# Weight fetches, the X split of odd groups and the gate blocks, moved to other places of a hand-written order

## The chip, the cores and the metric

The kernel runs on one NeuronCore of a Trainium2 chip. The metric is the time of one execution on the device, in microseconds. The core has five engines, each with its own queue of instructions, worked off in order: TensorE (PE, matmuls, with its weight loads shown as PEld), VectorE (DVE), ScalarE (ACT), GpSimd (POOL) and SyncE (SP), which here issues nearly all transfers (DMAs). An instruction waits in its queue until the semaphores say that its inputs are written and its output buffer has been read; what stands behind it in the same queue waits as well.

## The reference

Two branches read the same x (2048 tokens, 512 columns, float32) and are mixed by a gate for each token:

```python
qkv = (x @ wqkv).reshape(B, S, 3, H, Dh)          # H = 32 heads of Dh = 16
scores = einsum("bhqd,bhkd->bhqk", q, k) * Dh ** -0.5
mask = (i - j >= 0) & (i - j < 256)               # causal, sliding window
a = (softmax(where(mask, scores, -1e9)) @ v) @ wo
b = (silu(x @ w_gate) * (x @ w_up)) @ w_down      # 1792 hidden columns
g = sigmoid((x * gate_w).sum(-1))
out = g * a + (1 - g) * b
```

## The kernel before

Every float32 product is made of three matmuls: each operand is split into a rounded part (hi) and the rest (lo), and hi x hi, hi x lo and lo x hi are added. A split is two instructions: a cast on one engine and a subtraction on another. For weights and for the projected Q and K (the X tiles) these are ACT and POOL, for w_down both are on DVE.

The heads are worked in 8 groups of four. After a prologue that makes V and the first groups' Q and K, the main loop runs over 128 slots `t`, 16 for each group, and one more; slot `t` holds one block of 128 keys of group `t // 16`. Each slot has four head steps `hd`. In a step PE does, for one head, the scores of the next group for the row maxima (stage1, L280), the scores of this group for the exps (stage2, L319), and three products of a projection (L230). DVE reduces the first to maxima (L282), ACT takes the exp of the second (L321) and POOL masks it (L323, L326). Group 7, from slot 112 (`g7`) on, has no stage1.

Four slots make a unit. In a unit PE makes two projections of 1024 tokens each, into the accumulators `pa` and `pb`: either both halves of the Q and K of a later group (`group_half`) or one gate and one up tile of the hidden layer (`gate_half`, `up_half`), whose results are kept in DRAM (`kept_h`, written at L547) and read again in the last phase. The first slot of a unit also holds some 86 small matmuls of av (exps times V, L343) after its second step, and so is longer. `finish` then normalises av on ACT (L358) and DVE and writes it out (od, issued by POOL).

Everything else is put into places by hand. `later(t, hd, f)` puts `f` behind the matmuls of step (t, hd), in the order in which it was called, and the order of the program is the order in each engine's queue. So a place has a time on PE; on SP, only the order against other issues counts. The places that matter here:

- `prepare` (L163, placed at L517 to L520): splits the weights that were fetched before (`PEND.pop(0)()`, cast L67 on ACT and subtraction L70 on POOL into `wh`, `wl`, two buffers each) and then issues the fetch of the next weights (`prefetch`, L75). There is one buffer `raw` for fetched weights, so that the issue on SP waits for POOL's subtraction of the split just before it. For weights whose first use is in slot t, the second of a unit, the split is at (t - 1, 1); for those of a unit's first slot, at (t - 2, 0) or as early as `wh` and `wl` are free.
- `group_half`, L550: ACT copies the accumulators to two `ev` buffers (a ring of five), and later splits them into the one pair of X tiles (`half`, casts L67 on ACT, subtractions L70 on POOL). `stack` (L263, L264) then issues 12 transfers from the X tiles to the Q and K tiles. The second half of a group can be split only when the first half's stack has read the X tiles.
- the gate: for each of 16 blocks of 128 tokens, `gate_fetch` (L594, SP) fetches the block of x to one of two buffers in turn, and `gate_block` (L597, DVE) multiplies it with gate_w and sums; the buffers are X tiles that no group needs any more. `gate_end` (L605 on, ACT and DVE) makes the gate of the sums.
- in group 7, `wd_early` fetches eight tiles of w_down (L75) to `ev` buffers, two in each unit, and splits them on DVE in the first slot of the next unit.
- `put_max` (L293 to L298) sends the row maxima by way of DRAM into the Q tiles: md on SP, and then q, which waits until md has landed.

At a unit's end DVE turns the accumulators of its projections into hidden tiles: two products for pa (L532) after two tanh of ACT (L529), and two for pb (L544). The next unit's matmuls need these accumulators again.

Of the kernel before, what the change touches and what calls it, by code (L numbers as in the profile page):

```python
# [19 lines left out]
NB = S // P  # L20
# [13 lines left out]
def gated_mix(ctx, tc, xT, xn, wqk, wv, wo, wgu, wd, gw, out):  # L34
# [70 lines left out]
    def halves_of(t):  # L105
        n = t.shape[-1] // 2
        return [t[:, :n], t[:, n:]]
# [49 lines left out]
    PEND = []  # L157
# [21 lines left out]
    with ExitStack() as A:  # L179
# [14 lines left out]
        def kept():  # L194
            return sm.tile([P, CH], F32, name="ev", bufs=EV)
# [3 lines left out]
        def x_pair(pool=None, name="x"):  # L199
            return tuple((pool or sm).tile([P, 2 * CH], F32R, name=f"{name}{w}", bufs=1) for w in ("hi", "lo"))  # L200

        def split_qk(g, hf, cc, raw):
            hi, lo = (t[:, cc * CH:(cc + 1) * CH] for t in X[g, hf])
            split(hi, lo, raw, *act)
# [53 lines left out]
        def stack(g, hf):  # L258
            for pr in range(2):
                q, k = (halves_of(t[g % 2][pr])[hf] for t in (QT, KT))  # L260
                hi, lo = (x[32 * pr:] for x in X[g, hf])
                for b, (qx, kx) in enumerate(((hi, hi), (hi, lo), (lo, hi))):
                    nc.sync.dma_start(q[b::4].bitcast(F32), qx[:32].bitcast(F32))  # L263
                    nc.sync.dma_start(k[b::4].bitcast(F32), kx[64:96].bitcast(F32))  # L264
# [3 lines left out]
        def stage1(g, qb):  # L268

            hf, b = divmod(qb, NB // 2)  # L270
            if b == 0:
                MX[g, hf] = sm.tile([P, 4, NB // 2], F32, name="mx")
            q0, k0 = qb * P, max(0, qb - 2) * P
            n = q0 + P - k0
            for hd in range(4):
                pr, j = divmod(hd, 2)
                r = slice(64 * j, 64 * j + 63)

                ps = ps2.tile([P, CH], F32, name="ps2") if g == 0 and pr else ps1.tile([P, CH], F32, name="ps1")
                nc.tensor.matmul(ps[:, :n], QT[g % 2][pr][r, q0:q0 + P], KT[g % 2][pr][r, k0:k0 + n],  # L280
                                 start=True, stop=True)
                mx = nc.vector.tensor_tensor_reduce(out=ps[:, :n], in0=ps[:, :n], in1=mask[:, 3 * P - n:],  # L282
                                                    scale=1.0, scalar=NEG, op0=ALU.add, op1=ALU.max,
                                                    accum_out=MX[g, hf][:, hd, b:b + 1])
                if g == 0:
                    BEHIND.append(mx)
                yield
# [198 lines left out]
        first = chain(*(stage1(0, b) for b in range(NB)))  # L486
# [5 lines left out]
        for n, turn in enumerate(turns):  # L492
            for m, _ in enumerate(turn, 3 * NK * n):
                at = [max(0, i - wait) * 2 * NB // (total - wait) for i in (m, m + 1)]
# [19 lines left out]
        def later(t, hd, *fs):  # L514
            AT.setdefault((t, hd), []).extend(fs)

        for n, key in enumerate(KEYS[:-1]):  # L517
            if n:
                t, free = FIRST[key], LAST.get(KEYS[n - 2], 0) + 1 if n > 1 else 0
                later(*((t - 1, int(n > 1)) if t % 4 else (max(t - 2, free), 0)), prepare)  # L520

        SIL = {}

# [26 lines left out]
        def group_half(t, g, hf):  # L550

            t0 = t + 3 + hf

            def done(ps):
                places = [kept(), kept()]
                for m in range(2):
                    later(t0, 2 * m, lambda m=m: nc.scalar.copy(places[m], ps[m]))

                def half(m):
                    if m == 0:  # L560
                        X[g, hf] = x_pair()
                    split_qk(g, hf, m, places[m])
                first = t0 + 3 * hf
                later(first, 3, lambda: half(0))
                later(first + 1, 1, lambda: half(1))
                later(max(first + 1, (g - 1) * NB) if hf else first + 1, 3, lambda: stack(g, hf))
            return done
# [17 lines left out]
        g7 = (G - 1) * NB  # L585
# [7 lines left out]
        def gate_fetch(b):  # L593
            nc.sync.dma_start(XG[2 + b % 2], xn[b * P:(b + 1) * P])  # L594

        def gate_block(b):
            nc.vector.scalar_tensor_tensor(XG[1], XG[2 + b % 2], 1.0, XG[0], op0=ALU.mult, op1=ALU.mult,  # L597
                                           accum_out=gate[:, b:b + 1])
# [9 lines left out]
            nc.vector.tensor_scalar(igate, gate, -1.0, 1.0, op0=ALU.mult, op1=ALU.add)  # L608

        pieces = [h for two in (QT[0], KT[0], QT[1], KT[1]) for t in two for h in halves_of(t)]  # L610
        later(g7 - 4, 1, gate_place)
        for b in range(NB):
            t = g7 - 4 + b // 4 * 4
            later(*((t, 1), (t + 1, 3))[b // 2 % 2], lambda b=b: gate_fetch(b))
            later(t + 1 + b // 2 % 2, 2 + b % 2, lambda b=b: gate_block(b))
        later(g7 + NB - 3, 0, gate_end)
        for m in range(NB // 2):
            wd_early(m)

# [17 lines left out]
        for t in range(G * NB + 1):  # L637
            g, i = divmod(t, NB)
# [216 lines left out]
```

## Time and profile before

| what | value |
|---|---|
| three runs, us | 834.81, 838.31, 838.81 (median 838.31) |
| the profiled execution, us | 840.53, span 838.8 |
| PE busy, share of the span | 98% |
| DVE, ACT, POOL busy | 63%, 48%, 42% |
| mean granted TensorE clock | 0.995 |
| ACT's X split waiting for stack transfers (k<-xhi) | 9.5 us in 5 waits |
| DVE's gate blocks waiting for their fetch (xlo<-xn) | 11.7 us in 9 waits |

A row of the timeline has the start in us from the span's start, the duration in us, the engine, the line, the operation, output<-inputs and, in brackets, how long the engine sat idle before it and what ended that. "x2" means two instructions shown as one. Rows with SPq are issues of transfers on SP; their duration is that of the issue, not of the transfer. A piece of the chain of waits has start, duration and what it was. A row of the windows has the stretch, its length, the busy time of PE, PEld, DVE, ACT and POOL (with counts), the granted clock, the DMA engines' share and GB/s.

### The profile page before, as it was taken

The numbers are of one execution on the slowest core, as the hardware profiler recorded it, in microseconds if no ns is written. First come the engines' busy times: TensorE is split into PE (matmuls) and PEld (weight loads), VectorE is DVE, ScalarE is ACT, GpSimd is POOL, SyncE is SP. The second block draws the span as 40 slices with busy tenths as digits, with TensorE's granted clock in tenths as the row PEclk, the third lists the DMA queues.
The fourth block names the chain that finished last, engine by engine and source line by source line (L and its number), as shares of the span: only waits on it lengthen the run. The fifth ranks groups of instructions, "written<-read, shape, count | busy, mean of one in ns | idle before, by whom it ended". The sixth has DMA issues, their size and how long they took to land.

```text
span 838.8 us, 21376 instructions
## 1 busy us (share of the span) xinstructions
PE 824.8 (98%) x8329; PEld 697.2 (83%) x8329; DVE 528.8 (63%) x1493; ACT 400.1 (48%) x831; POOL 352.9 (42%) x640
## 2 busy tenths in 40 slices
PE   8999999999999999999999999989999999999998
PEld 7888998888889878888889888867788888888886
DVE  6396787877787777787787688865665332321322
ACT  7323566565556565565556555544533312222231
POOL 7723456465446565455556545455431211011020
PEclk9999999999999999999999999998999999999999
DMA  8584424523514434242454252453466342251401
GB/s 288 166 234 128 127 86 112 162 78 114 154 57 134 114 119 145 59 150 74 112 161 134 71 170 82 140 173 111 164 213 208 108 126 75 81 159 43 157 15 50
DMA packets 52980, 105.98 MB, mean 126 GB/s; under 512 B 9936, under 2 KB 14672, under 8 KB 52880
## 3 DMA queue, kind: packets, MB, share of 16 engines
q1 hardware_dynamic: 48912, 90.73, 35.8%
q0 software_dynamic: 3968, 13.90, 4.6%
q8 instruction: 65, 1.06, 0.5%
q14 instruction: 35, 0.29, 0.1%
HBM read 47.45 MB, written 31.98 MB: 95 GB/s over the span
## 4 chain that ended last, share of the span: by engine, by line
PE 89%; DMA 5%; SPq 2%; DVE 1%; issue 1%; ACT 1%; POOL 0%; DVEq 0%; ACTq 0%
PE pa L230 21%; PE pb L230 20%; PE pb L343 6%; PE ps L86 6%; PE ps L85 6%; PE ps L87 6%; PE ps L280 6%; PE ps L319 4%; PE ps L343 2%; DMA xlo<-xn 2%; PE pb L210 2%; PE pb L86 2%; PE pb L85 2%; PE pb L87 2%; DMA k<-xhi 2%; PE pa L737 1%
## 5 line engine op out<-in xcount | busy, mean ns | idle before, releaser
L282 DVE CUSTOM_DVE_ANT_0 ps<-ps,mask 128x384 f32<-128x384 f32 (+2 forms) x512 | 270.6, 539 | 114.3 <-PE ps L319 53.0
L321 ACT ACTIVATE pt<-ps 128x384 f32<-128x384 f32 (+2 forms) x512 | 238.0, 475 | 140.0 <-PE ps L280 70.8
L323 POOL TENSOR_SCALAR_AFFINE_SELECT pt<-pt 128x256 f32<-128x256 f32 x256 | 107.0, 418 | 220.3 <-ACT pt L321 218.1
L319 PE MATMUL ps<-q,k 64*128 64x384 f32 (+2 forms) x512 | 159.8, 331 | 0.0
L280 PE MATMUL ps<-k,q 63*128 63x384 f32 (+2 forms) x512 | 158.8, 330 | 0.8 <-DVE mx L282 0.8
L230 PE MATMUL pa<-xhi,wh 64*128 64x512 f32 x512 | 118.4, 399 | 3.9 <-DVE ev L532 3.8
L230 PE MATMUL pa<-xlo,wh 64*128 64x512 f32 x512 | 116.8, 395 | 0.0
L230 PE MATMUL pa<-xhi,wl 64*128 64x512 f32 x512 | 115.7, 392 | 0.0
L230 PE MATMUL pb<-xhi,wh 64*128 64x512 f32 x512 | 113.2, 394 | 0.0
L230 PE MATMUL pb<-xhi,wl 64*128 64x512 f32 x512 | 112.2, 392 | 0.0
L230 PE MATMUL pb<-xlo,wh 64*128 64x512 f32 x512 | 112.1, 391 | 0.0
L70 DVE TENSOR_TENSOR hl<-got,hh 128x512 fp32r<-128x512 f32 x51 | 43.3, 851 | 98.3 <-ACT hh L67 98.3
L280 PEld LDWEIGHTS ps<-k,q 63*128 63x128 f32 x512 | 88.7, 185 | 16.4 <-issue 5.7
L326 POOL TENSOR_SCALAR_AFFINE_SELECT pt<-pt 128x256 f32<-128x256 f32 x224 | 100.5, 449 | 0.0
L319 PEld LDWEIGHTS ps<-q,k 64*128 64x128 f32 x512 | 90.3, 184 | 4.8 <-issue 0.8
L343 PE MATMUL ps<-pt,vg 64*32 64x320 f32 (+4 forms) x1408 | 76.3, 350 | 3.1 <-ACT pt L321 3.1
L343 PE MATMUL pb<-pt,vg 64*32 64x320 f32 (+3 forms) x1360 | 78.1, 355 | 0.0
L282 DVE DVE_READ_ACCUMULATOR2_ANT mx<- 128x1 f32 x512 | 71.9, 140 | 0.0
L230 PEld LDWEIGHTS pa<-xhi,wh 64*128 64x128 f32 x512 | 62.5, 186 | 11.1 <-DVE ev L532 6.7
L343 PEld LDWEIGHTS pb<-pt,vg 64*32 64x32 f32 x1360 | 47.2, 107 | 27.2 <-DVE mx L282 7.3
L230 PEld LDWEIGHTS pa<-xhi,wl 64*128 64x128 f32 x512 | 61.9, 185 | 5.9
L230 PEld LDWEIGHTS pb<-xhi,wh 64*128 64x128 f32 x512 | 59.6, 185 | 5.6
(161 smaller groups left out, 1553.6 us busy)
## 6 DMA issues: line engine op xcount, KB each, us to landing
kept_h<-ev SPq DMA_DIRECT2D x52, 256.0 KB
got<-kept_h SPq DMA_DIRECT2D x51, 256.0 KB
od<-o POOLq DMA_DIRECT2D x32, 256.0 KB, 3.7
raw<-wgu SPq DMA_DIRECT2D x28, 256.0 KB
q<-xhi SPq DMA_DIRECT2D x56, 128.0 KB
k<-xhi SPq DMA_DIRECT2D x56, 128.0 KB
vd<-vs POOLq DMA_DIRECT2D x8, 672.0 KB, 4.7
vg<-vd SPq DMA_DIRECT2D x32, 168.0 KB
```

The costliest lines, as they stand in the source:

```text
L70: lo_eng.tensor_tensor(out=lo, in0=src, in1=hi.bitcast(F32), op=ALU.subtract)
L85: nc.tensor.matmul(ps, lh, rh, start=start and i == 0, stop=False, skip_group_check=skip)
L86: nc.tensor.matmul(ps, lh, rl, start=False, stop=False, skip_group_check=skip)
L87: nc.tensor.matmul(ps, ll, rh, start=False, stop=stop and i == n - 1, skip_group_check=skip)
L230: mm = nc.tensor.matmul(ps[me], w[r], x[r], start=not second and i == 0, stop=bool(second) and i == n - 1)
L280: nc.tensor.matmul(ps[:, :n], QT[g % 2][pr][r, q0:q0 + P], KT[g % 2][pr][r, k0:k0 + n], start=True, stop=True)
L282: mx = nc.vector.tensor_tensor_reduce(out=ps[:, :n], in0=ps[:, :n], in1=mask[:, 3 * P - n:], scale=1.0, scalar=NEG, op0=ALU.add, op1=ALU.m ...
L319: nc.tensor.matmul(ps[:, :n], KT[g % 2][pr][r, k0:k0 + P], QT[g % 2][pr][r, k0:k0 + n], start=True, stop=True)
L321: BEHIND.append(nc.scalar.activation(pt[:, j, :n], ps[:, :n], AF.Exp, scale=SCALE))
L323: nc.gpsimd.affine_select(out=pt[:, :, :P], in_=pt[:, :, :P], pattern=[[0, 2], [1, P]], compare_op=ALU.is_ge, fill=0.0, base=0, channel_mu ...
L326: nc.gpsimd.affine_select(out=pt[:, :, 2 * P:], in_=pt[:, :, 2 * P:], pattern=[[0, 2], [-1, P]], compare_op=ALU.is_ge, fill=0.0, base=-1, ...
L343: nc.tensor.matmul(AV[g, c][h][32 * j:32 * j + 32, q0 - c * CH:q1 - c * CH], VG[4 * g + kb // 4][o, kb % 4, 17 * j:17 * j + 32], PT[g, kb, ...
```

## The change

Three edits, all to places.

1. At L517 the split and the next fetch get places of their own. The fetch moves from directly behind the split to (t, 0), where the split is at (t - 1, 1), and to two steps behind the split where that is in step 0.
2. In `group_half` the second half's two casts and subtractions move one slot later for odd groups. Their stack stays at the start of the next group's 16 slots.
3. The gate blocks, four to a unit, move from the units that start in slots 108, 112, 116 and 120 to those of 112, 116, 120 and 124. With u for the start of the unit, blocks and fetches stood and stand at:

| block of the unit | fetch before | block before | fetch after | block after |
|---|---|---|---|---|
| a | (u, 1) | (u+1, 2) | (u-1, 0) | (u+1, 0) |
| b | (u, 1) | (u+1, 3) | (u-1, 1) | (u+1, 2) |
| c | (u+1, 3) | (u+2, 2) | (u+1, 1) | (u+2, 1) |
| d | (u+1, 3) | (u+2, 3) | (u+1, 3) | (u+2, 3) |

`gate_place`, which fetches gate_w, moves from slot 108 to 110, and `gate_end` from (125, 0) to (127, 0). The w_down fetches and splits keep their places, at (u+1, 2) and (u+2, 2) and in the next unit's first slot.

```diff
@@ places of the weights
             if n:
                 t, free = FIRST[key], LAST.get(KEYS[n - 2], 0) + 1 if n > 1 else 0
-                later(*((t - 1, int(n > 1)) if t % 4 else (max(t - 2, free), 0)), prepare)
+                at = (t - 1, int(n > 1)) if t % 4 else (max(t - 2, free), 0)
+                later(*at, lambda: PEND.pop(0)())
+                later(*((t, 0) if t % 4 else (at[0], 2)), prefetch)
@@ def group_half
-                first = t0 + 3 * hf
+                first = t0 + (3 + g % 2) * hf
                 later(first, 3, lambda: half(0))
                 later(first + 1, 1, lambda: half(1))
                 later(max(first + 1, (g - 1) * NB) if hf else first + 1, 3, lambda: stack(g, hf))
@@ the gate
-        later(g7 - 4, 1, gate_place)
+        later(g7 - 2, 1, gate_place)
         for b in range(NB):
-            t = g7 - 4 + b // 4 * 4
-            later(*((t, 1), (t + 1, 3))[b // 2 % 2], lambda b=b: gate_fetch(b))
-            later(t + 1 + b // 2 % 2, 2 + b % 2, lambda b=b: gate_block(b))
-        later(g7 + NB - 3, 0, gate_end)
+            t, n = g7 + b // 4 * 4, b % 4
+            later(t + (-1, -1, 1, 1)[n], (0, 1, 1, 3)[n], lambda b=b: gate_fetch(b))
+            later(t + (1, 1, 2, 2)[n], (0, 2, 1, 3)[n], lambda b=b: gate_block(b))
+        later(g7 + NB - 1, 0, gate_end)
```

## The prediction

> **What bounds the kernel now.** I read the page first, then the chain of waits in order of time, then the timelines of each engine around the pieces of that chain that are not TensorE.
>
> ```profile
> span 838.8 us, 21376 instructions
> PE 824.8 (98%) x8329; PEld 697.2 (83%) x8329; DVE 528.8 (63%) x1493; ACT 400.1 (48%) x831; POOL 352.9 (42%) x640
> PEclk9999999999999999999999999998999999999999
> PE 89%; DMA 5%; SPq 2%; DVE 1%; issue 1%; ACT 1%; POOL 0%; DVEq 0%; ACTq 0%
> ```
>
> TensorE (PE) sets the pace, so a wait is worth only what it costs PE. The 98% hides stalls, since matmul ends are modelled. The start of a slot's first score matmul (L319) is the better clock: a unit is one long slot, which carries the av matmuls, and three short ones of about 3.5 us. I give positions as (slot, head step); the first slot of group 7, the last, is 112.
>
> The chain names two kinds of transfer. The first is a stack transfer (k<-xhi), on which ScalarE (ACT) waits with the X split of an odd group's second half:
>
> ```profile
> 175.33 0.33 PE L319 MATMUL ps<-q,k 64*128 64x384 f32 x1
> 181.50 0.34 PE L319 MATMUL ps<-q,k 64*128 64x384 f32 x1
> ...
> 192.07 0.33 PE L319 MATMUL ps<-q,k 64*128 64x384 f32 x1
> 199.91 0.33 PE L319 MATMUL ps<-q,k 64*128 64x384 f32 x1
> ...
> 326.74 0.33 PE L319 MATMUL ps<-q,k 64*128 64x384 f32 x1
> 334.58 0.33 PE L319 MATMUL ps<-q,k 64*128 64x384 f32 x1
> ...
> 460.17 0.33 PE L319 MATMUL ps<-q,k 64*128 64x384 f32 x1
> 467.68 0.33 PE L319 MATMUL ps<-q,k 64*128 64x384 f32 x1
> ```
>
> Slot 24 is an undisturbed long slot: 6.17 us. Slots 28, 60 and 92 (groups 3, 5, 7) take 7.84, 7.84 and 7.51: together 4.7 us over.
>
> The second kind is the gate blocks' transfer (xlo<-xn), which holds VectorE (DVE), and DVE frees the accumulators (pa) that the next unit's first matmuls need:
>
> ```profile
> 400.50 0.33 PE L319 MATMUL ps<-q,k 64*128 64x384 f32 x1
> 410.67 0.33 PE L319 MATMUL ps<-q,k 64*128 64x384 f32 x1
> ...
> 533.65 0.33 PE L319 MATMUL ps<-q,k 64*128 64x384 f32 x1
> 545.38 0.34 PE L319 MATMUL ps<-q,k 64*128 64x384 f32 x2
> 560.81 0.42 PE L319 MATMUL ps<-q,k 64*128 64x384 f32 x2
> 564.66 0.79 PE L230 MATMUL pa<-xhi,wh 64*128 64x512 f32 x1 [3.43 <-DVE ev L532]
> 573.02 0.35 PE L319 MATMUL ps<-q,k 64*128 64x384 f32 x2
> 582.51 0.44 PE L319 MATMUL ps<-q,k 64*128 64x384 f32 x1
> 588.79 0.33 PE L319 MATMUL ps<-q,k 64*128 64x384 f32 x2
> 598.15 0.36 PE L319 MATMUL ps<-q,k 64*128 64x384 f32 x2
> 605.17 0.33 PE L319 MATMUL ps<-q,k 64*128 64x384 f32 x2
> ```
>
> Unit 108: its three short slots take 545.38 - 533.65 = 11.73 us; its twin in group 4, unit 76, needs 410.67 - 400.50 = 10.17 for the same work. That is 1.5 over. Slot 116: 12.21 us against 6.28 in slot 120, 5.9 over: PE stood still for 3.43 us and then ran slow. Slot 124: 7.02, 0.7 over. So the last group loses 6.6, and all known stalls add to 4.7 + 1.5 + 6.6 = 12.8 us.
>
> **The change part by part.**
>
> X split of odd groups, one slot later. The two casts and two subtractions are the same; only their place moves, from (27,3) and (28,1) to (28,3) and (29,1) in group 3.
>
> ```profile
> 194.54 0.62 ACT L67 CAST xhi<-ev 128x512 fp32r<-128x512 f32 x1 [2.45 <-DMA k<-xhi]
> 198.18 0.59 ACT L358 COPY o<-ps 128x512 f32<-128x512 f32 x1 [1.74 <-PE ps L343]
> 198.66 0.50 ACT L321 ACTIVATE pt<-ps 128x384 f32<-128x384 f32 x1
> ```
>
> ACT stood for 2.45 us until the last of 12 stack transfers landed; the exps behind it on ACT kept the ps buffers and so PE. In its new place the cast comes behind the copy at 198.18 and two exps, four microseconds after that landing, or over two once the stall's 1.7 us is taken off. The wait is gone: 4.7 us. The new place costs at worst its overrun of a step: 0.62 + 0.50 against 3.48/4 = 0.87, 0.25 us, twice for three groups, 1.5 us if the two ps buffers did not take it up. The first half's casts already sit in such short slots beside an unstalled PE, so I take 0. The stack of that half starts at (32,3) as before; the evacuated tiles are held one slot longer, and the ring of five next needs them at slot 35. Even groups keep their place; I count nothing there.
>
> Weight transfers. An issue on SP has no slot of its own, only its turn in SP's queue, so the move matters only where it passes another issue. Most move past nothing. Behind a split at (24,1), (44,1) and so on the next weights now go out after the maxima transfers and the 12 stack issues instead of before. They leave some 8 us later, with seven or so slots to spare until their split; I take 0. The stack gains no more than the 0.4 us that one issue takes (the row of 554.87 below), because the maxima ahead of it wait for DVE in any case. In the last group the fetches at (112,1) and (120,1) no longer stand before the gate's fetches and wait there for POOL's subtraction.
>
> Gate blocks. Unit 108 loses four blocks (0.8 us of DVE each) with their waits: 1.5 us back. Units 112 to 124 get four each: a and b at the head of the second slot and its middle, c and d in the third. Fetches a and b go out two slots ahead. But c's buffer is free only after a, d's after b, and between the two issues SP now has a w_down fetch and two kept_h writes. The price of d comes from unit 120 as template, with times from its start at 582.51:
>
> ```profile
> 587.87 0.69 DVE L360 TENSOR_TENSOR o<-pb,o 128x512 f32<-128x512 f32 x1 [2.61 <-ACT o L358]
> 588.93 0.77 DVE L70 TENSOR_TENSOR k<-ev,k 128x512 fp32r<-128x512 f32 x1
> 595.48 0.83 DVE L597 SCALAR_TENSOR_TENSOR xhi<-xlo,xhi 128x512 f32<-128x512 f32 x1 [0.51 <-DMA xlo<-xn]
> 598.13 1.27 DVE L532 SCALAR_TENSOR_TENSOR ev<-ev,pa 128x512 f32<-128x512 f32 x2
> ```
>
> The two pieces of the chain that carry such a transfer, and SP's queue around them:
>
> ```profile
> 556.32 5.93 DMA xlo<-xn
> ...
> 593.63 3.67 DMA xlo<-xn
> ```
>
> ```profile
> 551.32 0.58 SPq L296 DMA_DIRECT2D md<-mtt  x1
> 553.85 0.98 SPq L298 DMA_DIRECT2D q<-md  x2
> 554.87 0.40 SPq L75 DMA_DIRECT2D ev<-wd  x1
> 555.31 0.91 SPq L547 DMA_DIRECT2D kept_h<-ev  x2
> 556.32 0.96 SPq L594 DMA_DIRECT2D xlo<-xn  x2
> ...
> 592.77 1.20 SPq L594 DMA_DIRECT2D xlo<-xn  x2
> ```
>
> DVE ends the second w_down split at +7.2 (588.93 + 0.77) in either kernel, held by the copy before 587.87. Block a then ends at +8.0 and c is issued, which lands 2.7 us later (592.77 to 595.48), at +10.7. SP goes on: c's issue 0.6, w_down 0.4, kept_h 0.9, so d leaves at +9.9. How long d takes lies between 3.67 us (the second of the pair of 592.77, issued behind one other transfer) and 5.93 us (that of 556.32, issued behind a w_down fetch and two kept_h writes). The second has the queue that d will have, so I stay near it: 5.3, and d lands at +15.2. Block d (0.8) and the two products (1.27) end at +17.25. PE wants pa at 598.15 + 0.3, +15.95. The stall is 1.3 us in slots 120 and 124; bounds 0 and 2.0.
>
> Unit 112 also has the maxima: SP holds from md (551.32) to q (553.85). Without the weights and gate fetches ahead of it md goes some 1.5 us earlier, but the weight fetch, 0.33 to issue and about 0.5 of queue, stands ahead of c. I take 2.2 for slot 116 (bounds 0.8 and 3.6). Unit 124 has no w_down fetch, which saves about a microsecond, but the gate's exp now stands on ACT ahead of the last two tanh and waits for block d, with the last exps and the transition behind it: 0.7 (0 to 1.5). Together 2.2 + 1.3 + 1.3 + 0.7 = 5.5 in place of 6.6: 1.1 us.
>
> A stall of 2.2 us is shorter than the one that slowed the clock; slots 28 and 60, 1.7 over, left it at full speed:
>
> ```profile
> 558.00:572.00 14.00, 10.57 (x112) 7.04 (x110) 5.10 (x10) 3.92 (x9) 2.97 (x7) 0.76 0.59 201
> ```
>
> In this window the granted clock was 0.76: 0.24 x 14 = 3.4 us lost. 2.2 is nearer 1.7 than 3.43, so no loss of clock is in the sum. In the Trainium skill, "TensorE: Matmul & The Clock Gate", Part 1 on the clock gate, the clock halves after a whole idle window of about 3.4 us, and the windows run freely. By that rule a stall of 2.2 us can never slow the clock, and my sum stays; at the upper bound of 3.6 it depends on the phase, and the rule would add the 3.4 us only in some executions.
>
> Sum: 4.7 + 1.5 + 1.1 = 7.3 us. Against the profiled execution's own 840.53 us (1.7 more than its span) that gives 833.2; against the median 838.31, 831.0. Of the runs before one stood at 834.81, so that 3.5 us come and go by themselves.
>
> **The rivals.**
>
> All waits go. If d lands at the lower bound, 9.9 + 3.7, DVE ends at +15.7 and nothing stalls: 838.3 - 12.8 = 825.5. For it: fewer issues stand between SP and the fetches than before; against it: each fetch c and d still waits for a block of its own unit.
>
> One loss of clock stays. Slot 116 stalls 3.6 and loses 3.4 more: 4.8 worse than the forecast, 835.8. For it: the queue ahead of c in unit 112 is the longest of the four, and that slot is where it happened.
>
> The moved split brings nothing, because the stacks go out later too or POOL, with its subtractions in short slots, holds the next av: 831.0 + 4.7 = 835.7. Against it: the landing at 194.3 is well ahead of the new place.
>
> Slower: the fetch of d is slower in every unit than that of 556.32 was in one. Its place is d's turn behind w_down and kept_h; it decides once the transfer takes over 7.4 us, for then each of the slots 116, 120 and 124 stands 3.4 us and loses clock, 5.9 each as slot 116 did. 17.7 + 0.7 against 6.6 is 11.8 lost; less 6.2 won elsewhere, 5.6 over: 843.9. For it: kept_h, w_down and the gate share one queue here in all four units. Against it: no transfer of a gate block in the chain took even 6 us.
>
> **How the numbers follow.** The forecast has 0.46 (its own range 828 to 834.5), all waits gone 0.20, one loss of clock 0.16, the split without effect 0.08, slower 0.10. A measurement tells about 0.5% from no change, 4.2 us: faster is under 834.1, slower over 842.5. Faster then holds most of the forecast, the first rival and a little of the two at 835.7: 0.70; slower 0.09; the rest, 0.21, is the same. The range reaches from 824.5, the first rival with 0.4 us for the stacks of two or three groups besides, to 837.0, past the two rivals at 835.7.
>
> **What would show it.** Slots 28, 60 and 92 near 6.2 us, and no wait of ACT's xhi cast on k<-xhi in odd groups. Unit 108's short slots near 10.2. In slots 116, 120, 124 a wait of PE's pa matmuls on DVE ev of 1 to 2 us each, DVE's block d released by xlo<-xn each time, and no dip in the clock row. The prediction is wrong if slot 116 still takes 12 us, if the weight split waits for its late fetch, or if PE waits in slots 29 or 30.

## The result, and the profile after

| | before | after |
|---|---|---|
| runs, median (lowest to highest), us | 838.53 (834.81 to 839.73), 6 runs | 830.1 (829.66 to 832.56), 6 runs |
| the profiled execution, us | 840.53, span 838.8 | 829.82, span 828.1 |

The ratio is 0.9914, with a 95% interval from 0.989 to 0.9938: faster by 8.4 us between the medians, against the 7.3 of the sum. Two executions of the experiments, one of 2851.78 us with edit 1 alone and one of 4006.33 us with d's fetch earlier, were disturbed and are left out of the medians. The page of the changed kernel, its lines in the order in which those of before were shown:

```profile
span 828.1 us, 21367 instructions
PE 820.1 (99%) x8329; PEld 697.0 (84%) x8329; DVE 531.5 (64%) x1493; ACT 399.8 (48%) x831; POOL 351.3 (42%) x640
PEclk9999999999999999999999999999999999999999
PE 93%; DMA 2%; DVE 1%; SPq 1%; issue 1%; ACT 0%; POOL 0%; DVEq 0%
```

The engines do the same work. The chain, which had 5% in transfers and 2% in SP's queue, has 2% and 1%, and the clock row has lost its one 8. The timeline of PE, changed kernel, at the first score matmul of the slots that the prediction followed, with one pa matmul between:

```profile
192.27 0.33 PE L319 MATMUL ps<-q,k 64*128 64x384 f32 x1
198.44 0.33 PE L319 MATMUL ps<-q,k 64*128 64x384 f32 x1
...
324.04 0.33 PE L319 MATMUL ps<-q,k 64*128 64x384 f32 x1
330.19 0.33 PE L319 MATMUL ps<-q,k 64*128 64x384 f32 x1
...
456.19 0.33 PE L319 MATMUL ps<-q,k 64*128 64x384 f32 x1
462.36 0.33 PE L319 MATMUL ps<-q,k 64*128 64x384 f32 x1
...
528.26 0.33 PE L319 MATMUL ps<-q,k 64*128 64x384 f32 x1
538.43 0.34 PE L319 MATMUL ps<-q,k 64*128 64x384 f32 x2
553.70 0.44 PE L319 MATMUL ps<-q,k 64*128 64x384 f32 x2
554.86 0.49 PE L230 MATMUL pa<-xhi,wh 64*128 64x512 f32 x1 [0.72 <-DVE ev L534]
560.58 0.34 PE L319 MATMUL ps<-q,k 64*128 64x384 f32 x2
570.05 0.82 PE L319 MATMUL ps<-q,k 64*128 64x384 f32 x2
577.81 0.35 PE L319 MATMUL ps<-q,k 64*128 64x384 f32 x2
587.17 0.38 PE L319 MATMUL ps<-q,k 64*128 64x384 f32 x2
593.33 0.34 PE L319 MATMUL ps<-q,k 64*128 64x384 f32 x2
```

Differences of these starts, beside those of before. The last stretch goes from the start of slot 127 (as the others, from its first L319 in the trace) to the end of the span.

| stretch | before, us | after, us | gained |
|---|---|---|---|
| slots 28, 60, 92 | 7.84, 7.84, 7.51 | 6.17, 6.15, 6.17 | 4.7 |
| slots 109 to 111 | 11.73 | 10.17 | 1.6 |
| slot 116 | 12.21 | 6.88 | 5.3 |
| slot 120 | 6.28 | 7.76 | -1.5 |
| slot 124 | 7.02 | 6.16 | 0.9 |
| start of slot 127 to the end | 227.46 | 228.67 | -1.2 |
| slot 48 | 7.27 | 6.08 | 1.2 |

These add to 11.0 us, and the spans differ by 10.7. Slots 71 and 72 take back the difference: 9.98 us together before, 10.32 after, and 10.3 to 10.4 in every kernel below that has edits 1 and 2; the runs leave open why. Slot 48 was most likely a chance of the one profiled execution of before: every kernel below, those with a single edit too, has 6.09 to 6.10 there. Without it 9.8 us of the table are the change's, in this pair of executions.

How the first kind of stall went shows on ACT where slot 28 ends, in the timeline of the changed kernel:

```profile
196.69 0.59 ACT L358 COPY o<-ps 128x512 f32<-128x512 f32 x1 [2.66 <-PE ps L343]
198.36 0.61 ACT L67 CAST xhi<-ev 128x512 fp32r<-128x512 f32 x1
```

The cast, which had waited 2.45 us for the stacks, now comes after the copy and has no bracket: it waits for nothing. The waits by engine, changed kernel (engine, what it is to write and its line, what it waited for: us in total, times, longest):

```profile
DVE xhi L599 <- DMA xlo<-xn: 11.9, 8, 2.6
...
PE pa L230 <- DVE ev L534: 1.3, 2, 0.7
PE pa L343 <- POOL pt L323: 1.1, 1, 1.1
```

DVE waits for the gate's blocks as long as before (11.9 us against 11.7); what has gone is that PE waited for DVE behind it, 1.3 us now against 3.8, and the longest 0.7 against 3.4. (Edit 1 adds two lines, so that in the kernels that have it L534, L549, L596, L599 and L607 are what L532, L547, L594, L597 and L605 were.)

### The profile page after: what moved, and what is told of

The parts are those of the page before. It is cut to its first block, busy times and chain, and to the rows that moved or that the text cites. A ratio compares the mean times of both kernels' runs of the same rounds, so it can differ in the third digit from the quotient of the medians.

```text
span 828.1 us, 21367 instructions
## 1 busy us (share of the span) xinstructions
PE 820.1 (99%) x8329; PEld 697.0 (84%) x8329; DVE 531.5 (64%) x1493; ACT 399.8 (48%) x831; POOL 351.3 (42%) x640
## 4 chain that ended last, share of the span: by engine, by line
PE 93%; DMA 2%; DVE 1%; SPq 1%; issue 1%; ACT 0%; POOL 0%; DVEq 0%
PE pa L230 23%; PE pb L230 22%; PE pb L343 7%; PE ps L86 6%; PE ps L87 6%; PE ps L85 6%; PE ps L280 6%; PE ps L319 4%; PE pb L210 2%; PE ps L343 2%; PE pb L86 2%; PE pb L87 2%; PE pb L85 2%; DMA xlo<-xn 2%; PE pa L739 1%; PE pb L739 1%
## 5 line engine op out<-in xcount | busy, mean ns | idle before, releaser
L319 PE MATMUL ps<-q,k 64*128 64x384 f32 (+2 forms) x512 | 160.2, 331 | 0.0
L319 PEld LDWEIGHTS ps<-q,k 64*128 64x128 f32 x512 | 90.7, 184 | 5.7 <-issue 0.8
L343 PE MATMUL ps<-pt,vg 64*32 64x320 f32 (+4 forms) x1408 | 75.0, 346 | 0.0
L343 PE MATMUL pb<-pt,vg 64*32 64x320 f32 (+3 forms) x1360 | 73.9, 350 | 0.0
L343 PEld LDWEIGHTS pb<-pt,vg 64*32 64x32 f32 x1360 | 46.4, 106 | 28.0 <-DVE mx L282 7.3
```

Source lines behind the costliest of these rows:

```text
L319: nc.tensor.matmul(ps[:, :n], KT[g % 2][pr][r, k0:k0 + P], QT[g % 2][pr][r, k0:k0 + n], start=True, stop=True)
L343: nc.tensor.matmul(AV[g, c][h][32 * j:32 * j + 32, q0 - c * CH:q1 - c * CH], VG[4 * g + kb // 4][o, kb % 4, 17 * j:17 * j + 32], PT[g, kb, ...
```

## The experiments

Called 1, 2 and 3: the weight fetches two or three steps behind their split, the X split of odd groups one slot later, and the gate blocks in the last group. My theory after the result: 2 gives the 4.7 us, 3 gives the rest, 1 gives nothing. The rival: 1 gives part of it, since it takes a waiting issue out of SP's queue ahead of the gate's fetches. Each kernel ran on one chip beside runs of the kernel before, whose medians on the chips lie within 1.2 us of each other; differences between kernels that ran on different chips carry that much doubt.

| kernel | median, us (lowest to highest) | before, us | ratio [95%] |
|---|---|---|---|
| 1 alone | 833.57 (832.4 to 835.23) | 838.9 | 0.9941 [0.9921, 0.9961] |
| 1 alone, again | 834.22 (832.28 to 836.05) | 837.78 | 0.9947 [0.9926, 0.9967] |
| 2 alone | 832.08 (831.31 to 833.71) | 838.9 | 0.9924 [0.9897, 0.9951] |
| 3 alone | 835.69 (833.89 to 838.23) | 838.9 | 0.997 [0.9953, 0.9986] |
| 2 and 3 | 829.38 (828.57 to 829.76) | 838.9 | 0.9888 [0.9863, 0.9913] |
| 1 and 2 | 827.8 (827.56 to 830.65) | 837.78 | 0.9885 [0.9843, 0.9927] |
| 1, 2 and 3, again | 829.85 (828.97 to 830.56) | 837.78 | 0.9899 [0.9866, 0.9931] |
| fetch d a step earlier | 827.93 (826.79 to 827.97) | 838.05 | 0.9874 [0.9848, 0.9899] |
| end of the gate later | 829.39 (829.24 to 830.15) | 838.05 | 0.9897 [0.9876, 0.9918] |
| three buffers | 825.81 (825.67 to 826.08) | 838.05 | 0.9854 [0.9829, 0.9878] |
| three buffers, end later | 825.06 (824.99 to 825.82) | 838.05 | 0.9846 [0.9825, 0.9867] |
| three buffers, old places | 827.04 (826.62 to 827.5) | 838.94 | 0.9858 [0.983, 0.9885] |

The slots that differ, from the starts of L319 in each kernel's trace, in us:

```
slot          before  1     2      3     2+3   1+2   1+2+3       d     end   three  three  three
                      again alone  alone             after/again first late  bufs   +late  old places
60            7.84  10.04   6.17   8.40  6.17  6.13  6.15/6.13   6.17  6.13  6.13   6.17   6.17
71 + 72       9.98   9.89  10.07   9.98  9.99 10.29 10.32/10.35  10.30 10.39 10.40  10.32  10.30
110 + 111     8.25   9.60   8.11   6.68  6.68  7.93  6.68/6.68   6.68  6.69  6.68   6.69   7.90
115           3.12   3.12   3.12   3.11  3.11  3.12  3.11/3.12   3.69  3.12  3.12   3.12   3.12
116          12.21   6.74  11.14   6.45  6.07  6.44  6.88/6.96   5.68  6.81  5.26   5.26   5.29
119           3.24   3.25   3.22   3.23  3.22  3.25  3.23/3.23   3.92  3.25  3.26   3.26   3.29
120           6.28   6.29   6.28   7.77  7.74  6.29  7.76/7.77   6.27  7.72  6.29   6.26   6.30
124           7.02   5.81   6.16   6.47  6.49  5.83  6.17/6.67   6.28  6.21  5.85   5.81   5.82
127 to end  227.46 227.45 227.35 229.12 228.66 227.38 228.67/.64 228.28 227.89 228.24 227.51 227.50
```

**Edit 1 alone.** Only L517 to L520 of the diff:

```diff
-                later(*((t - 1, int(n > 1)) if t % 4 else (max(t - 2, free), 0)), prepare)
+                at = (t - 1, int(n > 1)) if t % 4 else (max(t - 2, free), 0)
+                later(*at, lambda: PEND.pop(0)())
+                later(*((t, 0) if t % 4 else (at[0], 2)), prefetch)
```

> The kernel before with the moved weight fetches alone. Theory (each part works by itself: the X split gives 4.7 us, the gate's places the rest, the moved fetches next to nothing): 0 to 1.2 us faster than before, the 1.2 only if slot 48's stack wait (7.27 us against 6.1) went because the stack now stands ahead of the fetch. Slots 28, 60, 92 stay at 7.5 to 7.8, slot 116 near 12. Rival (the order on SP did the last group's part: the fetch at (112,1) no longer stands ahead of the gate fetches and the maxima): 3 to 5 us faster, slot 116 at 7 to 9 and no dip of the clock.

It took 833.57 us against 838.9, 5 us less by the ratio, so the theory that edit 1 gives nothing falls. The trace kept of it is that of the 2851.78 us and can't be read slot by slot. So it ran again on another chip:

> The moved weight fetches alone, once more, for a trace that can be read slot by slot. The time fell by 5 us where my theory gave at most 1.2. New theory (the rival of the first run): the fetch at (112,1) no longer stands ahead of the gate fetches and of md on SP, so the gate's fourth block comes 2 us or more earlier and slot 116 loses no clock: slot 116 at 7 to 9 us, slots 28, 60, 92 still at 7.4 to 8.4, the time 4 to 6 us under before. Other theory (the stack goes out earlier, and the X split waits less): slots 28, 60, 92 at 6.2 to 6.8, and slot 116 at 11 to 12.

834.22 against 837.78, ratio 0.9947: 4.4 us by the ratio. By the slots it is in slot 116, 12.21 to 6.74 (I had expected 7 to 9), and in slot 124, 7.02 to 5.81 (0.9 of these 1.2 are gone with edit 2 alone too). Slots 60 and 111 were longer in this one execution (10.04; 5.47 for 4.12), which at 836.05 lies 1.8 above its kernel's median. Slots 28 and 92, at 7.66 and 7.60, are much as before, so the other theory, that the X split waits less, is out. SP's issues in the last group, first the timeline of the kernel before, then that of edit 1 alone:

```profile
544.17 5.11 SPq L75 DMA_DIRECT2D raw<-wgu  x2
549.39 1.88 SPq L594 DMA_DIRECT2D xlo<-xn  x2
```

```profile
545.08 0.84 SPq L596 DMA_DIRECT2D xlo<-xn  x2
551.94 0.59 SPq L296 DMA_DIRECT2D md<-mtt  x1
553.95 0.99 SPq L298 DMA_DIRECT2D q<-md  x2
...
556.90 1.35 SPq L596 DMA_DIRECT2D xlo<-xn  x2
```

The subtraction on POOL that the issue of 544.17 waited for, in the timeline before:

```profile
547.65 1.28 POOL L70 TENSOR_TENSOR wl<-raw,wh 128x512 fp32r<-128x512 f32 x1 [0.19 <-ACT wh L67]
```

PE with edit 1 alone, where slot 116 begins:

```profile
562.99 0.42 PE L319 MATMUL ps<-q,k 64*128 64x384 f32 x2
564.00 0.49 PE L230 MATMUL pa<-xhi,wh 64*128 64x512 f32 x1 [0.60 <-DVE ev L534]
```

Before, the weight fetch stood in SP's queue until POOL had done the subtraction that frees `raw`; two gate fetches, the maxima and the second pair of gate fetches stood behind it. Counted from the start of slot 112 (545.38 before; 547.6 here, 15.4 ahead of 562.99), the first pair went out at +4.0 before and at -2.5 with edit 1, md at +5.9 and +4.3, the pair that decides at +10.9 and +9.3. PE's stall fell from 3.43 us to 0.60, and with it the loss of clock in this slot. Not all of these 2.8 us are the earlier issue. This is the first block of the deciding pair on DVE, before and with edit 1 alone:

```profile
562.28 0.91 DVE L597 SCALAR_TENSOR_TENSOR xhi<-xlo,xhi 128x512 f32<-128x512 f32 x1 [6.19 <-DMA xlo<-xn]
```

```profile
561.92 0.69 DVE L599 SCALAR_TENSOR_TENSOR xhi<-xlo,xhi 128x512 f32<-128x512 f32 x1 [3.98 <-DMA xlo<-xn]
```

It began at +16.9 before and at +14.4 with edit 1. Of these 2.5 us, 1.6 come from the issue; the rest is the transfer, 6.0 us from issue to block before and 5.0 here. (The last 0.3 of the 2.8 are the blocks, 0.91 against 0.69.) The faster transfer does not need the edit: with edit 2 alone, where the weight fetch stands as before, the pair left at +11.1 and took 4.8, and the stall was 2.28 us. So the order on SP is worth some 1.6 us of the stall, and with it the clock where a stall of the old length loses it.

**Edit 2 alone.**

```diff
-                first = t0 + 3 * hf
+                first = t0 + (3 + g % 2) * hf
```

> The kernel before with the later X split of odd groups alone. Theory: 4.7 us faster, slots 28, 60, 92 at 6.2 each, slots 29 and 30 unchanged at 3.48, everything in the last group as before. Rival (the split's new place costs in the short slots, or the wait goes on to the next reader): 0 to 3 us faster, with over 0.2 us more in slots 29 and 30.

0.9924, 6.4 us (4.1 to 8.6). Slots 28, 60 and 92 all have 6.17; slot 124 has 6.16 for 7.02, and slot 116 is still at 11.14. The interval takes in the 4.7 of one profile. That the median gain lies above it may be chance, or the length of this stall, which varies: without edit 2, slot 60 took 7.84, 8.40 and 10.04 in three kernels, the last with a loss of clock.

**Edit 3 alone.** The hunk of the diff from `gate_place` to `gate_end`, and nothing else:

```diff
-        later(g7 - 4, 1, gate_place)
+        later(g7 - 2, 1, gate_place)
...
-        later(g7 + NB - 3, 0, gate_end)
+        later(g7 + NB - 1, 0, gate_end)
```

> The kernel before with the new places of the gate alone. Theory: 3.5 to 6 us faster: 1.5 from unit 108, and slots 116, 120, 124 at 6.2 to 8 with the clock full, less 1.4 at the end. Rival (the order on SP did it): slot 116 still over 9 us with a dip of the clock, and the time within 1.5 us of before.

0.997, 2.5 us, less than the 3.5 to 6 that I expected. It mends slot 116 (6.45) and slots 110 and 111 (1.6 together), and pays 1.5 in slot 120 and 1.7 at the end; slot 60 took 8.40 in the profiled execution.

**Edits 2 and 3, without edit 1.** The changed kernel with

```diff
-                at = (t - 1, int(n > 1)) if t % 4 else (max(t - 2, free), 0)
-                later(*at, lambda: PEND.pop(0)())
-                later(*((t, 0) if t % 4 else (at[0], 2)), prefetch)
+                later(*((t - 1, int(n > 1)) if t % 4 else (max(t - 2, free), 0)), prepare)
```

> The changed kernel with the weight fetches back behind their splits. Theory: within 1.2 us of the changed kernel (830.1), on the slower side if slot 48 goes back to 7.3. Rival (the order on SP did the last group's part): 3 to 6 us slower than the changed kernel, with slot 116 over 9 us.

829.38, ratio 0.9888, where the changed kernel has 0.9914 and 0.9899: the intervals overlap. Slot 116 is even shorter, 6.07. Beside the other two, edit 1 adds nothing that can be told.

**Edits 1 and 2, without edit 3, and the changed kernel again beside it.** The first is the diff without the hunk of edit 3, the second the changed kernel unaltered.

> The changed kernel with the gate back in its old places (moved fetches and later X split only). If the moved fetches alone take the clock loss out of slot 116, this keeps nearly all of the gain: 828 to 831, and the gate's new places are worth 0 to 1.5 on top. If they work on the X split's stalls, which the later split removes too, it is where the later X split alone was, near 832 to 834, with slot 116 over 11.

> The changed kernel itself, on the same chip as the two others: 829.5 to 832.6 as in its first runs, and the measure for what each part left out costs.

827.8 without edit 3, 829.85 with it, on one chip; three of four runs of the first lie under 828 at a mean granted clock of 1.0, and one at 830.65 with 0.997, so the intervals overlap, but the slots say the same. By them edit 3 wins 1.2 us in slots 110 and 111 and loses 0.5 in slot 116, 1.5 in 120, 0.8 in 124 and 1.3 at the end, a net loss of 2.9; the spans are 826.2 and 828.9. So edits 1 and 3 mend the same stall, that of slot 116, and only 2 alone leaves it. That slot is 5.5 us shorter with edit 1 alone and 5.8 with edit 3 alone, and counts once. That is why the single gains, 5 + 6.4 + 2.5 = 14 us, are more than the 8.4 of all three.

**What edit 3 pays, and for what.** The next kernels alter the changed kernel in how the gate's blocks are fetched or used, to see whether the late fetches c and d are the price. First, d issued a step earlier:

```diff
-            later(t + (-1, -1, 1, 1)[n], (0, 1, 1, 3)[n], lambda b=b: gate_fetch(b))
+            later(t + (-1, -1, 1, 1)[n], (0, 1, 1, 2)[n], lambda b=b: gate_fetch(b))
```

> The changed kernel with the fetch of each unit's fourth gate block one step earlier, so that on SP it stands ahead of the w_down fetch and the two kept_h writes, not behind them; its block keeps its place. Theory (the rest of the stalls in slots 116 and 120 is the queue ahead of that fetch): it lands 3 to 4 us after its issue and over 1 us earlier in its unit, the stalls go, slots 116 and 120 near 6.2, and the time falls by 1 to 2.5 us against the changed kernel. Rival (the block is late because DVE shares something with POOL's weight subtraction, or because the third block is late): slots 116 and 120 stay at 6.9 to 7.8, no change.

827.93, 1.9 to 2.2 us less than the changed kernel has on other chips. Slots 116 and 120 go to 5.68 and 6.27, so the late d was behind both stalls (in slot 120 by way of POOL, as is shown under "Block d" below). But slots 115 and 119 grow by 0.6 and 0.7. ACT's timeline in this kernel:

```profile
552.85 0.60 ACT L531 ACTIVATE ev<-pa 128x512 f32<-128x512 f32 x1 [0.87 <-DMA kept_h<-ev]
...
568.67 0.60 ACT L531 ACTIVATE ev<-pa 128x512 f32<-128x512 f32 x1 [0.56 <-DMA kept_h<-ev]
```

The fetch passed the writes of the kept tiles in SP's queue, and now the tanh waits for such a write to free its buffer: about half of the stall (0.6 + 0.7 + 0.2 in slots 115, 119 and 123, of 1.2 + 1.5) moved a slot ahead.

Second, the end of the gate (L607 to L610) two steps behind the last slot rather than at the start of slot 127:

```diff
-        later(g7 + NB - 1, 0, gate_end)
+        later(g7 + NB, 2, gate_end)
```

> The changed kernel with the gate's end (exp, add, reciprocal) moved from (127,0) to (128,2), behind the last tanh, the last exps and the last products. Theory (the 1.47 us gap before the last av is ACT waiting in the gate's end for the last block, with the last exps behind it): the gap falls under 0.5 and the time by 0.8 to 1.4 us against the changed kernel. Rival (the last block itself holds DVE and so the accumulators): the gap stays over 1 us.

829.39. The end is 0.8 us shorter (228.67 to 227.89), and PE has no wait there any more, as expected; the median is 0.5 to 0.7 lower than that of the changed kernel, where I expected 0.8 to 1.4, and the intervals overlap.

Third, three buffers for the fetched blocks in place of two, the product written over its input, so that c and d no longer wait for a and b and can be issued a slot earlier:

```diff
-            nc.sync.dma_start(XG[2 + b % 2], xn[b * P:(b + 1) * P])
+            nc.sync.dma_start(XG[1 + b % 3], xn[b * P:(b + 1) * P])
...
-            nc.vector.scalar_tensor_tensor(XG[1], XG[2 + b % 2], 1.0, XG[0], op0=ALU.mult, op1=ALU.mult,
+            nc.vector.scalar_tensor_tensor(XG[1 + b % 3], XG[1 + b % 3], 1.0, XG[0], op0=ALU.mult, op1=ALU.mult,
...
-            later(t + (-1, -1, 1, 1)[n], (0, 1, 1, 3)[n], lambda b=b: gate_fetch(b))
+            later(t + (-1, -1, 0, 1)[n], (0, 1, 0, 1)[n], lambda b=b: gate_fetch(b))
```

> The changed kernel with three buffers in turn for the gate's x instead of two: the product is written over its input, which frees the tile that took it. The third block's fetch goes out at the unit's start, the fourth's directly behind the first block, ahead of w_down and kept_h. Theory: no block waits for its fetch by more than 0.5 us, slots 116, 120 and 124 are near 6.2, the gap before the last av shrinks too, and the time falls by 2 to 3.5 us against the changed kernel, to 826.6 to 828.1. Rival: as for the fourth fetch put first, no change.

825.81, 4.0 to 4.3 us under the changed kernel, more than expected. Slots 116, 120 and 124 take 5.26, 6.29 and 5.85, and no other slot is more than 0.1 longer for it. These are the undisturbed lengths: slot 116 has 5.26, not the 6.28 of slot 120 that the prediction measured it by. The trace says why: slot 116 holds 64 matmuls of av (L343), as the second unit of each group does, and slot 120 holds 96; the number for all is not some 86. Slots 36, 68 and 100, with 64 too, take 5.56 to 5.57 us in the kernel before.

> The three buffers and the later gate's end together. Theory: 2.2 to 4 us less than the changed kernel, and at most 0.7 less than three buffers alone, since the last block is then early enough for the gate's end to wait for nothing. If the two causes were independent the gains of the two single runs would add up.

The last two edits shown, both together: 825.06, the best of all, 0.75 less than three buffers alone where I expected 0.7 at most. The waits of PE in this kernel, all of them (the one left is in the prologue):

```profile
PE pa L185 <- POOL ident masks.py:199: 1.4, 1, 1.4
```

Last, the rival to edit 3 itself: with three buffers, are the old places as good? (`gate_place` and `gate_end` go back to (108, 1) and (125, 0) as well.)

```diff
-            t, n = g7 + b // 4 * 4, b % 4
-            later(t + (-1, -1, 0, 1)[n], (0, 1, 0, 1)[n], lambda b=b: gate_fetch(b))
-            later(t + (1, 1, 2, 2)[n], (0, 2, 1, 3)[n], lambda b=b: gate_block(b))
+            t = g7 - 4 + b // 4 * 4
+            later(*((t + 1, 2) if b % 4 == 3 else (t, 1)), lambda b=b: gate_fetch(b))
+            later(t + 1 + b // 2 % 2, 2 + b % 2, lambda b=b: gate_block(b))
```

> Moved fetches and later X split, the gate blocks in their old places (units 108 to 120), with three buffers in turn: the third block's fetch goes out with the first two, the fourth's behind the first block, ahead of w_down and kept_h. Theory (early fetches decide, the places matter little): slots 110 and 111 within 0.2 of 3.35, slots 116, 120, 124 near 5.3, 6.3 and 5.8, no late gate's end: 825 to 826.5, level with three buffers in the new places. Rival (the old places cost by themselves, as four blocks stand beside the maxima's work of DVE in unit 108): slots 110 and 111 still 0.4 us or more over in sum, and 826.5 to 828.

827.04. Its slots 110 and 111 take 7.90 together against 6.69; everything behind them is as in the best kernel. In the old places four blocks stand beside the maxima on DVE, PE waits 0.46 us for such a maximum in slot 110, and the earlier fetches do not help that. So the new places are worth 1.2 us by the slots (2.0 between the medians, on two chips, and the intervals of the ratios overlap), once the fetches are early.

## Why the prediction was right, and where it was not

**The X split** was right in mechanism, place and size: ACT's cast waits for nothing, the slots are at 6.15 to 6.17, the sum is the 4.7 named, PE has no wait in slots 29 and 30, and the rival of a split without effect is out. What one profile could not show is how much this stall varies; alone it gave 6.4 us by the ratio.

**Unit 108** was right: 10.17, as named, 1.6 for 1.5. The old places with three buffers bear the cause out, DVE's blocks beside the maxima: early fetches alone leave 1.2 of the 1.6.

**Weight transfers** are the step that was wrong. "I take 0" stood for the fetches of the other groups. For those at (112,1) and (120,1) I had seen that they no longer stand ahead of the gate's and wait for POOL, but gave this no term of its own: it is only a part of what edit 3 gains in slot 116, as md going 1.5 us earlier. Alone it is worth 4.4 to 5 us, more than edit 3 alone (2.5). md went 1.6 us earlier in its slot, so the mechanism and that size were right, but I did not follow it to the stall of slot 116 in its old place, where the same 1.6 us at the issue saves the clock as well.

**The last group** was to gain 1.1; by the table it gained 3.5 (5.3 - 1.5 + 0.9 - 1.2). The total came out nearer, 8.4 for 7.3, since the profiled execution of before was 2 us above its median; that nearness is luck. Two terms were mis-sized. The old excess of slot 116 was 12.21 - 5.26 = 6.95, not 5.9, because slot 120 is no twin of it, with 96 av matmuls for 64; slot 124's was 7.02 - 5.81 = 1.2, not 0.7. And the new stalls, over the undisturbed lengths, are 1.6, 1.5, 0.4 and 1.2 us for 2.2, 1.3, 1.3 and 0.7: their sum 4.7 for 5.5, each within its bounds. PE's waits on DVE that I had named for slots 116, 120 and 124, of 1 to 2 us each, are 0.72, 0.62 and none. And the gain was credited to the wrong edit: beside the others, edit 3 costs some 2 us between medians (2.9 by the slots), since edit 1 had already mended slot 116.

**Block d.** The pieces of the chain of waits, changed kernel, that carry it in three of the four units:

```profile
548.38 4.50 DMA xlo<-xn
...
564.29 4.75 DMA xlo<-xn
...
596.46 3.89 DMA xlo<-xn
```

I took 5.3 between 3.67 and 5.93; that was too near the upper end. In unit 116, d leaves at +10.6 (564.29 - 553.70) rather than +9.9 and lands at +15.3, where I had +15.2. The excess of slot 120 then came out near the 1.3 by chance. DVE and POOL in the timeline of the changed kernel:

```profile
568.98 1.29 POOL L70 TENSOR_TENSOR wl<-raw,wh 128x512 fp32r<-128x512 f32 x1
```

```profile
562.96 0.65 DVE L599 SCALAR_TENSOR_TENSOR xhi<-xlo,xhi 128x512 f32<-128x512 f32 x1
...
569.14 1.68 DVE L599 SCALAR_TENSOR_TENSOR xhi<-xlo,xhi 128x512 f32<-128x512 f32 x1 [2.55 <-DMA xlo<-xn]
570.75 1.27 DVE L534 SCALAR_TENSOR_TENSOR ev<-ev,pa 128x512 f32<-128x512 f32 x2
```

Block d, which takes 0.65 when alone, took 1.68 because it began while POOL's subtraction ran: 1.0 of the 1.5 us lost in slot 120. Edit 3 puts it at the place of the weight split, which I had not looked at. In five executions with this place (edit 3 alone, edits 2 and 3, the changed kernel twice, the later end) the block began 0.16 to 0.51 us into the subtraction, ended 0.55 us behind it each time, and slot 120 took 7.72 to 7.77. In slot 116 POOL may have held block d as well: it took 1.23 us there (552.97 to 554.20) while POOL's masks ran to 553.65.

**The end.** The gate's end did what was feared for 0.7 us, with 1.2. The timeline of ACT in the changed kernel, and then of PE:

```profile
601.53 0.22 ACT L607 ACTIVATE gate<-gate 128x16 f32<-128x16 f32 x1 [0.71 <-DVE xhi L599]
601.65 1.06 ACT L531 ACTIVATE ev<-pa 128x512 f32<-128x512 f32 x2
602.61 0.44 ACT L321 ACTIVATE pt<-ps 128x128 f32<-128x128 f32 x2
```

```profile
603.86 0.43 PE L343 MATMUL pa<-pt,vg 64*32 64x320 f32 x1 [1.07 <-POOL pt L323]
```

The exp of the gate waits for the last block, the tanh and the last exps stand behind it, POOL masks what they give, and PE stands 1.07 us ahead of the last av.

**The rivals.** "All waits go" is not what this change does, but it is what three buffers do: 825.06, where that rival had 825.5. A loss of clock in slot 116 did not come in the profiled execution, nor the slower case: none of the three transfers of d in the chain took more than 4.75 us. Two of the six runs took 832.56 us at a mean granted clock of 0.998 and 0.997, the other four 829.66 to 830.2 at 0.999 to 1.0. So some clock was probably lost in those two; their traces are not kept, and where is open.

**The clock.** No wait of PE in the last group is longer than 1.1 us in the profiled execution, so that it could not test the sentence "by that rule a stall of 2.2 us can never slow the clock". The experiments did, and it is wrong, as the last section shows. Had the stall of 2.2 come, "no loss of clock" would have been a gamble. The other reason that I gave, slots 28 and 60 at full speed with 1.7 us over, was no better: these 1.7 are several short waits. PE's waits in the kernel before:

```profile
PE ps L343 <- ACT pt L321: 3.1, 4, 1.0
```

None is longer than 1.0 us, so they say nothing of one stall of 2.2.

Nor does the kernel before lose the clock each time. Of its 43 executions beside the experiments, four have a mean granted clock of 1.0 and took 835.42 to 837.67 us; eight have 0.995, as the profiled one has, and took 838.37 to 842.47. So the 12.21 us of slot 116 belong to the longer ones, and part of what edits 1 and 3 win is won only where the clock would have been lost.

## What to carry to other kernels

Two edits that mend one stall do not add: price each beside the others, not only against the kernel before. A transfer whose issue waits for a buffer delays everything behind it in its queue, so follow the issue's delay to the engine that stands last before putting it at 0; and give a ring of fetched blocks one more buffer before you move its users. Compare a stalled slot with the same slot of a kernel that has no stall, not with its neighbour, and ask of a slot's excess whether it is one wait or several.

## What the runs showed of the hardware

**The clock was lost after far less than 3.4 us of idle PE.** PE's timeline with edit 2 alone, and the windows around it (the clock is the third figure from the end):

```profile
554.87 0.42 PE L319 MATMUL ps<-q,k 64*128 64x384 f32 x2
557.57 1.39 PE L230 MATMUL pa<-xhi,wh 64*128 64x512 f32 x2 [2.28 <-DVE ev L532]
```

```profile
552.00:557.20 5.20, 3.29 (x30) 2.98 (x26) 1.91 (x5) 3.49 (x8) 2.70 (x7) 1.00 0.85 293
557.20:564.00 6.80, 6.43 (x68) 3.71 (x72) 3.14 (x6) 0.00 (x0) 0.33 (x1) 0.50 0.53 192
564.00:571.00 7.00, 7.00 (x84) 6.24 (x67) 5.26 (x13) 3.93 (x9) 4.05 (x8) 1.00 0.22 63
```

An idle stretch of 2.28 us was followed by 6.8 us at half the clock: 3.4 us lost. With edit 1 alone, slot 60 did it after 1.51 us, and another stall of 1.66 us in the same execution did not; PE's timeline and then the windows:

```profile
329.42 0.71 PE L343 MATMUL ps<-pt,vg 64*32 64x320 f32 x1 [1.51 <-ACT pt L321]
...
545.77 0.44 PE L280 MATMUL ps<-k,q 63*128 63x384 f32 x1 [1.66 <-DVE mx L282]
```

```profile
329.50:333.00 3.50, 3.50 (x71) 2.19 (x78) 0.00 (x0) 0.76 (x2) 2.79 (x4) 0.51 0.25 97
...
540.00:550.00 10.00, 8.06 (x78) 6.31 (x86) 8.63 (x27) 4.65 (x12) 4.75 (x9) 1.00 0.53 180
```

The slowed stretch lasted about 3.4 us. On a grid of 3.41 us through its start at 329.5, the idle stretch of 1.51 us lies within one interval, while the one that ended at 545.77 has a boundary at 544.5 (329.5 + 63 x 3.413) and leaves no more than 1.3 us in either. With edit 2 alone the drop at 557.2 left 1.9 us of the 2.28 in the interval that ended there.

Within each trace the clock's drops and returns all lie on one such grid, so that each of the 13 traces with a clock can be divided into its own intervals. PE's idle time in some of them, by its rows, and the clock of the interval behind:

| interval, at full clock | PE idle in it, us | the next interval |
|---|---|---|
| before, 560.69 to 564.10 | 2.87 | half clock |
| edit 2 alone, 553.78 to 557.20 | 1.91 | half clock |
| edit 1 alone, 326.08 to 329.49 | 1.51 | half clock |
| edit 3 alone, 326.80 to 330.21 | 1.52 | full clock |
| edit 1 alone, 544.53 to 547.94 | 1.24 | full clock |

The 13 traces have 3145 intervals at full clock. PE was idle for 1.91 us or more in 15 of them (13 at the kernel's end), and each was followed by half the clock; it was idle for 1.41 us or less in 3128, and none of these was. The two between, at 1.5 us, went one each way. So here the clock drops once PE was idle for somewhere around 1.5 us, 44%, of such an interval. An idle stretch of that length costs the clock or not by its phase, and no run here set the phase.

In the Trainium skill, "TensorE: Matmul & The Clock Gate", Part 1 on the clock gate, the clock drops after at least one idle window of about 3.4 us, and the windows run freely. The free windows agree with these runs; a whole window of idleness does not, and here the measurement decides.

**A DVE instruction with two inputs stood behind POOL's.** Block d above took 1.68 us for 0.65 when it began within POOL's subtraction of 1.29 us, and ended 0.55 us after it (570.82 against 570.27). In the Trainium skill, "SBUF — State Buffer", the section on two separate sides says that a DVE operation with two inputs in SBUF and a GpSimd operation that reads SBUF take the same pair of ports in turn, and that the second is blocked for the whole of the first. The rows above agree, and so do others. In six more places (edit 1 alone, edit 3 alone twice, edits 2 and 3, the changed kernel again, the later end) a gate block began 0.32 to 0.90 us into such a subtraction, took 0.93 to 1.53 us and ended 0.55 to 0.56 us behind it. In the kernel before, one began 0.23 us ahead of the subtraction: the block took 0.69 us, and the subtraction 1.61.
